# A new order for the steps of attention, of slot 0 and of the expert tables

## The chip, the cores and the metric

The kernel runs on one core of a Trainium2 chip. A core has five engines with queues of their own: PE (TensorE, matmuls and transposes; PEld is its loading of weights), DVE (VectorE), ACT (ScalarE), POOL (GpSimd) and SP, which here only issues transfers. The engines run side by side, each through its own list of instructions, and wait for each other by semaphores. The metric is the device time of the program in microseconds, the median of three runs.

## The reference

Three layers in a row, all in float32:

```python
scores = scale * np.matmul(q, k.transpose(0, 1, 3, 2))      # 2 x 12 heads, 448 x 448, D = 64
scores = np.where(mask, -1000000000.0, scores)              # causal
attn = np.exp(scores - np.max(scores, axis=-1, keepdims=True))
attn = attn / (np.sum(attn, axis=-1, keepdims=True) + 1e-09)
x = np.matmul(attn, v)                                      # -> 896 tokens x 768
expert_idx = np.argmax(xn @ en.T / tau, axis=1)             # 8 experts, top 1
out[mask] = gate_w[mask, None] * (np.maximum(x[mask] @ w1[e], 0.0) @ w2[e])   # 768 -> 1024 -> 768
h = np.maximum(np.maximum(x @ w1, x @ w2), x @ w3)          # last layer, 768 -> 768
return h @ w_out
```

## The kernel before, in words

Attention works on 12 pairs of heads (0 to 9, a, b; six for each of the two batches). The two heads of a pair stand in partitions 0 to 63 and 64 to 127. Queries come in 7 blocks i of 64 rows; block i sees 64 (i + 1) key columns, and the blocks are put into four groups that share a PSUM bank each: SG = ((6,), (5, 0), (4, 1), (3, 2)). The order in which all engines' instructions are issued is written out by hand in SCHEDULE, a list of words, and `emit` (the loop over SCHEDULE[:-1]) turns each word into instructions. Since each engine runs its own list, a word's place matters only against the other words of its engine, and by what it waits for. The first letter is the pair, then:

- S, Z: scores of a group's first and second block (`scores`, L503). Each matmul takes 64 rows and 64 columns of the array, a quarter. Head j lies in rows 64 j and writes to columns 64 (j xor SWAP[i]): SWAP is 0 for groups 0 and 1 and 1 for groups 2 and 3, so that the former use one diagonal of the array's quarters and the latter the other. A letter at the end (a, b, t, h) names the PSUM bank's tag.
- K: the causal mask added by a matmul (`masks`, L511). M: the rows' maxima on DVE (`row_max`, L515). E: exponentials with row sums on ACT (`row_exp`, L522). R: reciprocals on DVE (`row_rec`, L527 and L528).
- N: normalisation of a block's rows (`nrm`, L532), on DVE, or on POOL with a p behind it.
- T: transposes of the probabilities in 14 blocks of 128 x 128, in four steps (`ptr`, L542); t copies them out, on ACT (s) or DVE (v) (`ptr_out`, L476 or L478).
- A0 to A3: probabilities times values (`av`, L580 to L590). A0 to A2 use all 128 rows and half of the columns for each head, A3 only rows 0 to 63. a copies the output out, X transposes it to tokens (L599), x copies that out (s or v) and stores it on POOL's queue (L605).
- q scales the keys, L and V load on SP.

Words without a pair are steps that occur once: EA (norms of the expert embeddings on ACT, with two loads of activation tables, L143 and L144), ET, GA to GS1 and G4, G5 (logits of the experts), C0 and C1 (choice of experts for each batch, on DVE, L641 to L646), F1 to F3 (the first expert to run), XG (gather of its tokens), LW (a small transfer that holds the weights back until the gather has landed), L0, L1, L11, L13 (weights of slot 0), W (splits of these weights on ACT and DVE, L261 and L263), X0, X4 (transposes of slot 0's tokens) and H (slot 0's first layer, L272). The last string orders the tables of all further slots and slot 0's second layer (Y, L979): cnt, rk and iv are matmuls, P0 and P1 transposes of slot 0's hidden values (L328), sel, pb, A0 and A1 (here one-hot rows) and others are small DVE steps, J is the first layer of slot 1. Behind that the order is that of loops: up to 15 slots of 128 tokens, each with one expert, and then the last layer. None of that part is touched.

Of the kernel before, what the change touches and what calls it, by code (L numbers as in the profile page):

```python
# [15 lines left out]


SCHEDULE = (
    "0qv 0S0a 0S3 0S2b 0K0 0M0 0E0 0Z3 0K3 0M3 0S1b 0Z1 0Z2 0K2 0K1 1qv 0M2 0E3 4L 1S0a 1S3a 1Z3 1K3 0E2 0M1 1K0 1M0 0E1 1E0 1S2 1S1 1Z1 1K1 1Z2 1K2 5L 2qv 2S0b 2S3b 2Z3 2K0 2K3 2S2a 2S1 1M1 1E1 2Z2 2K2 0R 0N1p 1M3",
    "1E3 0N0 1M2 1E2 0N3 2Z1 2K1 0N4 0N2p 0T0t 0N5p 0N6 0T2 0t0s 3qs 0t2s 0T3h 0t3s 2M1 3S0 3S2 1R 3Z2 1N4p 2M3 2E3 3K2 1N3 0T1 2M2 2E2 0t1s 3S3h 1N2 1N1p 2M0 3K0 3M0 1N5p 3S1b 3Z3 3Z1 2E0 3K3 3M3 2E1 0A0a 0A2 0A1",  # L20
    "3M2 1N6p 1N0 2R 2N0p 2N5p 0A3 4V 2N1 6L 2N6p 1T0 1T2b 1t0v 4qs 1T3t 0as 1t2v 3E3 2N2 3K1 3M1 3E2 1t3v 2N3p 5qv 1T1 1t1s 2N4 4S0h 4S3a 3E1 4Z3 4K3 4M3 1A0t 1A2 3E0 1A1 3R 3N0p 3N3p 1A3 1av 5V 3N1p 4S2a 4K0 5S0b 4Z2",
    "2T0t 2T3t 2T1b 4M0 EA 2t0v 2T2t 2t3s 3N4p 6qv 2t2v 3N2p 4K2 4M2 4E3 3N5p 5S3 7L 7qv 4S1 2t1s 5Z3 5K3 4E2 5K0 4Z1 4K1 4M1 2A0a 2A1 3N6 2A2 5M0 4E0 4E1 2A3 6V 2as 3T0t 3T2h 3T1 3t0s 5M3 3T3t 5S1b 5E3 4R 4N3p 4N1p 4N5p",
    "5S2a 5Z2 3t2v 5E0 3t1v 5Z1 5K1 4N4p 5K2 5M1 6S0 6S3h 6Z3 5M2 3t3s 5E1 5E2 8L 6S1 4N6 4N0p 8qs 6S2b 6K3 6Z2 4N2 6Z1 6K1 6M1 6K0 6M0 6K2 3A0a 3A1 3A2 5R 5N4p 3A3 4T0 4T3b 7V 9L 6M3 5N0 5N1 3as 5N2p 4T1t 4t0s",
    "5N5p 5N3 4T2 4t3s 6E3 7S0b 4t2s 7S2a 7Z2 7K2 4t1v 4A0t 4A2 4A1 5N6p 7S3a 6E0 6M2 7K0 8S0 6E1 6E2 9qs 7M2 7Z3 7K3 6R 6N2p 6N3 4A3 8K0 8V aL 6N0 5T0h 5T2b 6N6 5t0s 6N1p 6N5p 8M0 7M3 5t2s 7M0 5T1t 5t1s 0Xh",
    "7S1b 7Z1 7E2 7K1 5T3t 5t3v 7E3 6N4p 5A0a 0xs 5A1 7E0 5A2 6T0h 6T1 8S2b 7M1 EM 7E1 8S1 7R 7N2p 6t1s 7N6 6t0s 7N5p 8Z2 8K2 6T3b 6t3s 6T2 7N3 1Xh 8Z1 8K1 8E0 aqv 1xs 7N4p 5A3 9S0 8S3b 8Z3 6t2s 8K3 8M2 6A0a 6A1",
    "8M1 8E2 8E1 6A2 8M3 9K0 9M0 7N1p 9V bL 8E3 ET 2Xh 7T0t 2xs 7t0s 3X 7T3b 7t3s GA 4as 9S1b 5as 8R 8N4p 6A3 aV 8N3 9Z1 9K1 GB 8N1p 7N0 7T2 4Xt 3xs GE0 9M1 7t2s 6as 7T1b GS0 9E0 7t1s 5Xt C0",
    "8N5p 7A0a 7A2 8N6p 4xs 8N2 F1 8T0 9E1 6Xt 9S3 9Z3 9K3 8t0s 7A3 7A1 9S2a 9Z2 9K2 F2 8N0p 6xs 9M2 7as 5xs F3 bV bqs RE 9M3 7Xt 8T3 8T2h XG 8t3v 9E2 8t2s 8T1t 8t1s aS0b aS2a aZ2 aK2 aK0 aS1a aS3b aZ3 aM2 aZ1 aK1",
    "aM0 9E3 bS0 9R bS2h bZ2 aE2 bS3 aM1 9N2p 9N0 9N6p 9N5 bZ3 bK3 aE0 9N3 aE1 9N1 aK3 aM3 9N4 bK2 7xs LW 8A0a 8A1 8A2 aE3 9T0b bM2 9t0s aR aN5p aN4 9T1t aN1p bK0 L0 8A3 9t1s aN0 8as bM0 9T2 9t2v X4 X4h X4l X0 X0h 9T3",
    "9t3v bE2 bE0 X0l bM3 bE3 bS1 bZ1 bK1 bM1 bE1 aN2 9A0a 9A1 9A2 aN6 L1 9A3 9as 8Xt W000h aN3p bR aT0t aT2b aT3t bN3 at3s at2s W001h bN5p bN2 bN0 at0s bN6 bN1 aT1 at1s GC 9X 8xv W010h GE1 bN4 bT0 bT2b bT1t bT3 W011h",
    "W010l aA0t aA1 bt1s W000l aA2 bt3v H00 aA3 W011l W021h bt2v aas GS1 G4 W001l aX W020h W020l H01 H04 H10 W030h bt0s W030l bA0a bA1 W031h W101h bA2 W021l 9xv W101l bA3 bav H02 H03 H05 L11 H13 W031l W100h G5 W100l W121h",  # L30
    "W121l W120h axs R0 H11 H12 H14 W110h L13 W120l C1 bXt bxs W110l",
    "rk ro cnt n8p rr g87 ge nb8 ks8 pre8 H15 rks B0 P0 U02 jj sb8 A0 sbo P0h P0l Y00 R1 Y10 W111h sl sl2 sel pb W131h P1 A1 pp iv Y11 Y13 nsf flg idx Y12 Y01 Y02 nsc P1h W130h P1l Y03 Y05 Y04 W130l inc st2 U03 st1 st3 st4 U11 st5 ti0 st6 W111l U10 Y06 xg1 x0 st7 x0h ti1 W131l RG x0l Y07 Y15 WS0 U00 Y16 U13 U01 q6 U12 x4 Y14 Y17 q3 q4 q5 x4h x4l q7 q8 q9 qb qc S1 qd qa qe qf B1 n8 J00 J10 J11 J02 J01 J03 J04 J05 J12 J14 r0 qh0 qg qh2 p0 qh1 gg p0h gx gs0 J13 J15 gs1 WS1 of0 of1 of2 y0 y1 p0l of3 of4 ti2 r1 RG1",
)


# [1132 lines left out]
```

## Time and profile before

| | |
|---|---|
| median of 3 runs (lowest, highest) | 471.49 us (471.2, 472.02) |
| profiled execution: its own time, its span | 473.37 us, 471.7 us |
| TensorE's mean granted clock | 0.999 of full speed |
| busy: PE, DVE, ACT, POOL | 459.0, 319.1, 269.1, 76.0 us |
| first score matmul, last step of pair b (X) | 5.74 us, 103.37 us |
| first matmul of slot 1 (J00) | 117.85 us |

The profile is that of one execution; all starts are in microseconds from the start of its span. The times of a group of instructions are durations from start to end, and those of neighbours overlap, since the engines are pipelined; what a stretch of an engine costs is read from start to start. In a line of the timeline, instructions of one form that lie close are merged (x12), and the bracket at the end gives the idle time in front and what ended it.

### The profile page before, as it was taken

Reading aid. Unit: us, or ns where it says so; the run is one execution under the profiler, and the core shown is the slowest. Engines: PE = TensorE matmul, PEld = TensorE weight load, DVE = VectorE, ACT = ScalarE, POOL = GpSimd, SP = SyncE. Lnnn points to the kernel's source line nnn. Section 1 sums busy time; section 2 is a strip of 40 time slices with the busy share of each in tenths; the row PEclk is TensorE's granted clock in tenths of the full one; section 3 lists DMA queues with packets and bytes.
Section 4 is the critical chain, followed back from the end, with each engine's and each line's share of the span. In section 5 each row is a group of like instructions: output and inputs, shape, how many; then the busy total and the mean of one; then the engine's idle time right before and its main releaser. Section 6 shows DMA issues by size and latency. Waiting matters only on the chain. (4 is left out here: it accounts for less than half of the span.)

```text
span 471.7 us, 9404 instructions
## 1 busy us (share of the span) xinstructions
PE 459.0 (97%) x3266; PEld 406.4 (86%) x3266; DVE 319.1 (68%) x642; ACT 269.1 (57%) x564; POOL 76.0 (16%) x101
## 2 busy tenths in 40 slices
PE   7999999999999999999999999999999999999994
PEld 6777777788899898998998987989989989899993
DVE  4987668887446794533978955898989889840000
ACT  5998878957627895335888954544444353410000
POOL 3877756111010000000000000000000000001111
PEclk9999999999999999999999999999999999999999
DMA  7444345931158891217999903844534330000111
GB/s 256 157 136 134 123 138 167 350 141 55 36 196 326 300 374 44 103 34 287 358 337 361 362 7 142 332 140 152 175 137 146 123 135 0 0 1 33 68 68 68
DMA packets 18175, 76.65 MB, mean 163 GB/s; under 512 B 2362, under 2 KB 5434, under 8 KB 18114
## 3 DMA queue, kind: packets, MB, share of 16 engines
q1 hardware_dynamic: 15410, 65.84, 39.1%
q0 software_dynamic: 2400, 9.83, 5.8%
q8 instruction: 27, 0.44, 0.4%
q10 hardware_dynamic: 304, 0.25, 0.2%
q14 instruction: 34, 0.28, 0.2%
...
## 5 line engine op out<-in xcount | busy, mean ns | idle before, releaser
L973 PE MATMUL pm<-x2h,dwh 128*128 128x512 f32 (+1 forms) x204 | 74.1, 363 | 0.0
L974 PE MATMUL pm<-x2l,dwh 128*128 128x512 f32 (+1 forms) x204 | 74.0, 363 | 0.0
L975 PE MATMUL pm<-x2h,dwl 128*128 128x512 f32 (+1 forms) x204 | 74.0, 363 | 0.0
L979 PE MATMUL l<-w2h,hh 128*128 128x384 f32 x160 | 55.3, 346 | 0.7 <-ACT hh L208 0.7
L979 PE MATMUL l<-w2l,hh 128*128 128x384 f32 x160 | 54.1, 338 | 0.0
L243 DVE TENSOR_TENSOR w1l<-raw,w1h 128x768 fp32r<-128x768 f32 x40 | 36.0, 953 | 21.8 <-ACT w1h L242 16.5
L532 POOL TENSOR_SCALAR prb<-prb,smq 128x384 f32<-128x384 f32 (+6 forms) x45 | 44.3, 1000 | 19.7 <-DVE smq L528 11.2
L175 ACT CAST dwh<-dt_t 128x768 fp32r<-128x768 f32 (+1 forms) x20 | 15.5, 774 | 53.5 <-DVE dt_t L174 53.5
L979 PE MATMUL l<-w1h,xhp 128*128 128x512 f32 x109 | 44.0, 404 | 0.0
L979 PE MATMUL l<-w1l,xhp 128*128 128x512 f32 x109 | 43.1, 395 | 0.0
L522 ACT ACTIVATE prb<-pss,smq 128x64 f32<-128x64 f32 (+6 forms) x84 | 39.2, 494 | 5.7 <-DVE smq L515 3.9
L975 PEld LDWEIGHTS pm<-x2h,dwl 128*128 128x128 f32 x204 | 38.3, 188 | 4.0
L973 PEld LDWEIGHTS pm<-x2h,dwh 128*128 128x128 f32 x204 | 38.3, 188 | 4.0
L974 PEld LDWEIGHTS pm<-x2l,dwh 128*128 128x128 f32 x204 | 38.3, 188 | 4.0
L1119 POOL DMA_INDIRECT out_dram<-ob,sidx x7 | 6.8, 976 | 195.1 <-DVE ob L1118 195.1
L979 PE MATMUL l<-w2h,hl 128*128 128x384 f32 x160 | 36.6, 338 | 0.1
L515 DVE TENSOR_REDUCE smq<-pss 128x1 f32<-128x256 f32 (+6 forms) x84 | 30.8, 413 | 8.6 <-PE pss L511 8.5
L199 POOL DMA_INDIRECT xrp<-xd,idx x11 | 11.2, 1019 | 152.1 <-PE xtp L217 144.4
L243 DVE TENSOR_TENSOR w2l<-raw,w2h 128x768 fp32r<-128x768 f32 x40 | 35.3, 955 | 0.4 <-ACT w2h L242 0.4
L242 ACT CAST w2h<-raw 128x768 fp32r<-128x768 f32 x40 | 30.5, 841 | 4.7 <-SPq L352 2.6
L242 ACT CAST w1h<-raw 128x768 fp32r<-128x768 f32 x40 | 31.7, 853 | 0.0
L979 PEld LDWEIGHTS l<-w2h,hh 128*128 128x128 f32 x160 | 30.1, 188 | 1.6 <-ACT hh L208 1.0
(260 smaller groups left out, 1004.4 us busy)
## 6 DMA issues: line engine op xcount, KB each, us to landing
...
```

The costliest lines, as they stand in the source:

```text
L175: nc.scalar.copy(out=hi[:, c0:c1], in_=f)
L199: nc.gpsimd.indirect_dma_start(out=xrp, out_offset=None, in_=xd if i else xd[0:S], in_offset=bass.IndirectOffsetOnAxis(ap=idx[:, i:i + 1] ...
L242: nc.scalar.copy(out=hi[:, sl], in_=r[:, sl])
L243: nc.vector.tensor_tensor(out=lo[:, sl], in0=r[:, sl], in1=hi[:, sl], op=ALU.subtract)
L515: nc.vector.tensor_reduce(out=sms[p][:, 0, SC[i]:SC[i] + 1], in_=held["s", p, g][:, SO[i]:SO[i] + 64 * (i + 1)], axis=AX.X, op=ALU.max, ne ...
L522: nc.scalar.activation(out=prb[p % 2][:, poff[i]:poff[i] + n], in_=ps[:, SO[i]:SO[i] + n], func=AF.Exp, bias=sm[:, 0, SC[i]:SC[i] + 1], sc ...
L532: eng.tensor_scalar(out=r, in0=r, scalar1=sms[p][:, 2, SC[i]:SC[i] + 1], scalar2=None, op0=ALU.mult)
L973: nc.tensor.matmul(o, lhsT=lh, rhs=rh, start=first, stop=False)
L974: nc.tensor.matmul(o, lhsT=lh, rhs=rl, start=False, stop=False)
L975: nc.tensor.matmul(o, lhsT=ll, rhs=rh, start=False, stop=last)
L979: nc.tensor.matmul(o, lhsT=a, rhs=b, start=first and n == 0, stop=last and n == len(ops) - 1)
L1119: nc.gpsimd.indirect_dma_start(out=out, out_offset=bass.IndirectOffsetOnAxis(ap=sidx[:, t:t + 1], axis=0), in_=ob, in_offset=None)
```

## The change

SCHEDULE is replaced. Both lists hold the same 735 words apart from their last letters: 6 of the 84 normalisations change from POOL to DVE on balance (45 to 39 on POOL), copies change between ACT and DVE, and PSUM tags change. Nothing else in the kernel differs.

```diff
@@ -16,20 +16,19 @@
 SCHEDULE = (
-    "0qv 0S0a 0S3 0S2b 0K0 0M0 0E0 0Z3 0K3 0M3 0S1b 0Z1 0Z2 0K2 0K1 1qv 0M2 0E3 4L 1S0a 1S3a 1Z3 1K3 0E2 0M1 1K0 1M0 0E1 1E0 1S2 1S1 1Z1 1K1 1Z2 1K2 5L 2qv 2S0b 2S3b 2Z3 2K0 2K3 2S2a 2S1 1M1 1E1 2Z2 2K2 0R 0N1p 1M3",
-    "1E3 0N0 1M2 1E2 0N3 2Z1 2K1 0N4 0N2p 0T0t 0N5p 0N6 0T2 0t0s 3qs 0t2s 0T3h 0t3s 2M1 3S0 3S2 1R 3Z2 1N4p 2M3 2E3 3K2 1N3 0T1 2M2 2E2 0t1s 3S3h 1N2 1N1p 2M0 3K0 3M0 1N5p 3S1b 3Z3 3Z1 2E0 3K3 3M3 2E1 0A0a 0A2 0A1",
-    "3M2 1N6p 1N0 2R 2N0p 2N5p 0A3 4V 2N1 6L 2N6p 1T0 1T2b 1t0v 4qs 1T3t 0as 1t2v 3E3 2N2 3K1 3M1 3E2 1t3v 2N3p 5qv 1T1 1t1s 2N4 4S0h 4S3a 3E1 4Z3 4K3 4M3 1A0t 1A2 3E0 1A1 3R 3N0p 3N3p 1A3 1av 5V 3N1p 4S2a 4K0 5S0b 4Z2",
-    "2T0t 2T3t 2T1b 4M0 EA 2t0v 2T2t 2t3s 3N4p 6qv 2t2v 3N2p 4K2 4M2 4E3 3N5p 5S3 7L 7qv 4S1 2t1s 5Z3 5K3 4E2 5K0 4Z1 4K1 4M1 2A0a 2A1 3N6 2A2 5M0 4E0 4E1 2A3 6V 2as 3T0t 3T2h 3T1 3t0s 5M3 3T3t 5S1b 5E3 4R 4N3p 4N1p 4N5p",
-    "5S2a 5Z2 3t2v 5E0 3t1v 5Z1 5K1 4N4p 5K2 5M1 6S0 6S3h 6Z3 5M2 3t3s 5E1 5E2 8L 6S1 4N6 4N0p 8qs 6S2b 6K3 6Z2 4N2 6Z1 6K1 6M1 6K0 6M0 6K2 3A0a 3A1 3A2 5R 5N4p 3A3 4T0 4T3b 7V 9L 6M3 5N0 5N1 3as 5N2p 4T1t 4t0s",
-    "5N5p 5N3 4T2 4t3s 6E3 7S0b 4t2s 7S2a 7Z2 7K2 4t1v 4A0t 4A2 4A1 5N6p 7S3a 6E0 6M2 7K0 8S0 6E1 6E2 9qs 7M2 7Z3 7K3 6R 6N2p 6N3 4A3 8K0 8V aL 6N0 5T0h 5T2b 6N6 5t0s 6N1p 6N5p 8M0 7M3 5t2s 7M0 5T1t 5t1s 0Xh",
-    "7S1b 7Z1 7E2 7K1 5T3t 5t3v 7E3 6N4p 5A0a 0xs 5A1 7E0 5A2 6T0h 6T1 8S2b 7M1 EM 7E1 8S1 7R 7N2p 6t1s 7N6 6t0s 7N5p 8Z2 8K2 6T3b 6t3s 6T2 7N3 1Xh 8Z1 8K1 8E0 aqv 1xs 7N4p 5A3 9S0 8S3b 8Z3 6t2s 8K3 8M2 6A0a 6A1",
-    "8M1 8E2 8E1 6A2 8M3 9K0 9M0 7N1p 9V bL 8E3 ET 2Xh 7T0t 2xs 7t0s 3X 7T3b 7t3s GA 4as 9S1b 5as 8R 8N4p 6A3 aV 8N3 9Z1 9K1 GB 8N1p 7N0 7T2 4Xt 3xs GE0 9M1 7t2s 6as 7T1b GS0 9E0 7t1s 5Xt C0",
-    "8N5p 7A0a 7A2 8N6p 4xs 8N2 F1 8T0 9E1 6Xt 9S3 9Z3 9K3 8t0s 7A3 7A1 9S2a 9Z2 9K2 F2 8N0p 6xs 9M2 7as 5xs F3 bV bqs RE 9M3 7Xt 8T3 8T2h XG 8t3v 9E2 8t2s 8T1t 8t1s aS0b aS2a aZ2 aK2 aK0 aS1a aS3b aZ3 aM2 aZ1 aK1",
-    "aM0 9E3 bS0 9R bS2h bZ2 aE2 bS3 aM1 9N2p 9N0 9N6p 9N5 bZ3 bK3 aE0 9N3 aE1 9N1 aK3 aM3 9N4 bK2 7xs LW 8A0a 8A1 8A2 aE3 9T0b bM2 9t0s aR aN5p aN4 9T1t aN1p bK0 L0 8A3 9t1s aN0 8as bM0 9T2 9t2v X4 X4h X4l X0 X0h 9T3",
-    "9t3v bE2 bE0 X0l bM3 bE3 bS1 bZ1 bK1 bM1 bE1 aN2 9A0a 9A1 9A2 aN6 L1 9A3 9as 8Xt W000h aN3p bR aT0t aT2b aT3t bN3 at3s at2s W001h bN5p bN2 bN0 at0s bN6 bN1 aT1 at1s GC 9X 8xv W010h GE1 bN4 bT0 bT2b bT1t bT3 W011h",
-    "W010l aA0t aA1 bt1s W000l aA2 bt3v H00 aA3 W011l W021h bt2v aas GS1 G4 W001l aX W020h W020l H01 H04 H10 W030h bt0s W030l bA0a bA1 W031h W101h bA2 W021l 9xv W101l bA3 bav H02 H03 H05 L11 H13 W031l W100h G5 W100l W121h",
-    "W121l W120h axs R0 H11 H12 H14 W110h L13 W120l C1 bXt bxs W110l",
-    "rk ro cnt n8p rr g87 ge nb8 ks8 pre8 H15 rks B0 P0 U02 jj sb8 A0 sbo P0h P0l Y00 R1 Y10 W111h sl sl2 sel pb W131h P1 A1 pp iv Y11 Y13 nsf flg idx Y12 Y01 Y02 nsc P1h W130h P1l Y03 Y05 Y04 W130l inc st2 U03 st1 st3 st4 U11 st5 ti0 st6 W111l U10 Y06 xg1 x0 st7 x0h ti1 W131l RG x0l Y07 Y15 WS0 U00 Y16 U13 U01 q6 U12 x4 Y14 Y17 q3 q4 q5 x4h x4l q7 q8 q9 qb qc S1 qd qa qe qf B1 n8 J00 J10 J11 J02 J01 J03 J04 J05 J12 J14 r0 qh0 qg qh2 p0 qh1 gg p0h gx gs0 J13 J15 gs1 WS1 of0 of1 of2 y0 y1 p0l of3 of4 ti2 r1 RG1",
+    "0qv 0S0b 0S2a 0Z2 0K0 0M0 0K2 0M2 0S1 0Z1 0S3 1qv 0Z3 0K3 4L 0K1 1S0 1S2b 1Z2 1K2 0E0 0E2 1S3b 1Z3 0M3 0E3 0M1 0E1 1K0 1M2 1M0 2qs 1E0 1K3 1M3 1S1 1Z1 1K1 1E3 5L 1E2 0R 0N0p 2S0h 2S3 2Z3 2K3 2S1a 2S2 2Z2 1M1 0N4p",
+    "0N5 0N1 2Z1 0N3 1E1 2K2 2K0 2K1 0N2 0N6 3qv 0T0b 0T1 0t0s 2M3 0t1s 1R 1N0p 1N4p 2M1 0T2b 0t2s 1N3p 0T3t 0t3s 2M0 1N2 2E1 2M2 0A0 0A1 0A2 4qv 2E0 1N1 2E3 0A3 4V 6L 0av 3S0 3S3b 1N5p 3S2a 3Z3 3K3 1N6 3K0 3Z2 3K2 3M2",
+    "2E2 1T0 3M3 2R 2N3p 5qs 1T2t 2N4p 1t0s 3E2 2N1 3M0 1T1b 2N0 1T3t 1t2s 3S1a 3Z1 1t3s 3K1 3E0 4S0h 4S3a 3M1 3E1 4Z3 4K3 4K0 4S1 1t1v 2N5p 3E3 4M3 4S2 4Z2 4K2 1A0 1A1 4M2 2N2p 1A2 3R 3N6p 3N2p 2N6 4Z1 4K1 1A3 1av 5V",
+    "7L 2T0b 2T3 EA 3N1p 2T2t 2t2s 2t0v 2t3v 2T1b 2t1v 4E3 4M1 5S0b 5S2a 5Z2 5K2 3N3 4M0 4E0 2A0 2A2 3N4p 2A1 5K0 2A3 5M2 3N5 6V 8L 3T0 3T3t 3N0p 2av 4E2 6qv 3T2h 3T1t 4E1 3t3v 3t0s 5M0 5E0 4R 4N0p 4N3p 4N2 4N1p 4N6 5S1",
+    "5S3b 5Z3 3t1s 5Z1 5K1 5M1 5K3 4N4 3t2s 6S0a 5E1 6S2 6Z2 5E2 6K0 5M3 5E3 6K2 3A0 3A2 3A1 3A3 7V 7qs 4T0t 6M0 6M2 4t0v 4N5p 4T2 4t2v 4T1t 4T3h 6S1b 6S3 3as 6E2 4t1s 5R 5N2p 4t3s 6Z3 5N3p 5N6 7S0b 7S2a 6E0 8qv 6K3 6M3",
+    "5N4 5N1p 6E3 7Z2 9L 5N0 6Z1 6K1 6M1 5N5 4A0t 4A2 9qv 7S1 7S3h 7K2 7M2 7Z3 6E1 6R 7K0 7M0 6N1p 6N3 7Z1 7K1 6N4 7K3 4A3 5T0t 5T3 5t0s 5t3s 6N2 5T2b 7E2 6N6p 7M1 4A1 5t2s 6N0 EM 5T1t 8V 5t1s 0Xa 0xs 6T0 8S0 8S2b 8Z2",
+    "8K0 aL 7E0 5A0a 7E1 5A2 7M3 7E3 5A1 6t0v aqs 1Xa 7R 6N5p 7N0 7N6 6T3t 7N5 7N3p 6t3s 6T2h ET 1xs 7N2 6T1t 6t1v 5A3 8S3b 7N1p 9V bL 8S1a 8K2 8M0 6t2s 8E0 8M2 8Z3 8Z1 8K1 8M1 7N4p 8K3 8M3 GA 2Xt 8E2 7T0t 4av 5av 7T1b",
+    "2xs 8E3 3Xt 8E1 GB GE0 bqv 8R 8N2p 8N0 8N1p 6A0 8N4 6A1 6A2 7t1s 3xs 8N3p 9S0a 9S2a 7t0s 9Z2 9S1b 9K2 9K0 9Z1 6A3 9K1 8N6 8N5p 9M0 aV 6as GS0 4X 7T2t 9M1 7T3t 7t2s 5Xt C0 F1 F2 8T0t 4xs 9E1 7A0h 8t0s 6X 7A1 7t3s",
+    "7A2 9E0 9M2 6xs 5xs 9S3 9Z3 9K3 7A3 bV 7as F3 RE 9M3 8T3 8T2t 8T1b 8t2v XG 8t3s 9E2 8t1s aS0 aS3a aZ3 aK3 aM3 9E3 aE3 aK0 8A0t 8A2 8A1 aM0 aS1b 9R 9N2p 9N4p 9N3 9N6 9N0 9N1 aS2h aZ2 aZ1 aK1 aM1 aK2 aM2 aE0 8A3 8as",
+    "bS0 bS3a bS2 bK0 bS1a aE1 bM0 aE2 bZ2 bK2 bZ3 9N5 bZ1 bK1 bM1 aR aN2 LW bK3 aN4 bM3 9T0b 9T2t 9t0s aN6 aN1p 9T3h 9t3s 9T1b X4 9t2s aN3p bM2 9t1s X4h X4l 7Xh aN5 9A0t 9A1 9A2 9A3 9av bE1 bE3 bE2 aT0b aT3b at3s at0v",
+    "aT1 8Xt aN0 aT2 at1v at2v bE0 9X bR bN1p bN2p X0 7xs X0h GC aA0a bN5 aA1 L0 bN6 X0l bN4p aA2 W001h W001l aA3 bN3 W000h W000l GE1 W011h W011l bN0 W010h aas GS1 bT0 bT1t bT3b bt0v bt1v W010l 8xs H00 bT2 aXt bt2v G4",
+    "W021h W020h W020l W031h H01 bt3s 9xv H04 H02 bA0a bA1 bA2 W031l bA3 W021l W030h L1 L11 W100h W030l W100l bas H03 H05 W101h G5 R0 H10 H13 H11 H12 W101l axs W121h C1 W120h bXa H14 W121l W120l W110h L13 W110l bxs",
+    "cnt n8p rk ro H15 g87 rr rks nb8 ge pre8 ks8 B0 U02 P0 sb8 sbo sl jj P0h W130h sl2 P0l Y10 Y11 sel pp A0 U10 pb A1 inc st2 Y00 U11 nsf R1 iv idx Y13 flg nsc Y12 W111h st1 Y01 st3 st4 st5 P1 P1h ti0 W111l W131h Y02 Y03 st6 st7 P1l ti1 Y05 Y04 Y06 xg1 x0 U03 W130l W131l x0h RG Y15 Y07 x0l WS0 q6 Y16 U00 Y14 x4 U01 Y17 x4h U12 U13 q3 q4 q5 x4l q7 q8 q9 qb qc S1 qd qa qe qf B1 n8 qh0 J10 J11 J00 J02 J01 J03 J04 J05 r0 J12 J14 qg qh2 qh1 p0 p0h gg J13 gx gs0 gs1 J15 WS1 of0 y0 p0l of1 of2 of3 of4 ti2 y1 r1 RG1",
 )
```

## Rows read from the trace of the kernel before

**Rows 1.** The page's line of busy times, and PE's busy tenths in 40 slices.

```profile
PE 459.0 (97%) x3266; PEld 406.4 (86%) x3266; DVE 319.1 (68%) x642; ACT 269.1 (57%) x564; POOL 76.0 (16%) x101
...
PE   7999999999999999999999999999999999999994
```

**Rows 2.** Stretches: length; busy us PE, PEld, DVE, ACT, POOL (instructions); clock, DMA share, GB/s.

```profile
0.00:20.00 20.00, 16.80 (x250) 13.14 (x250) 13.31 (x43) 14.89 (x51) 10.96 (x29) 1.00 0.61 206
20.00:40.00 20.00, 19.56 (x304) 15.66 (x300) 17.92 (x50) 18.61 (x61) 14.88 (x17) 1.00 0.41 126
40.00:60.00 20.00, 20.00 (x279) 15.18 (x278) 12.17 (x39) 17.91 (x59) 15.01 (x16) 1.00 0.45 149
60.00:80.00 20.00, 19.59 (x263) 15.40 (x260) 15.13 (x61) 15.87 (x48) 12.32 (x14) 1.00 0.41 122
80.00:100.00 20.00, 19.57 (x204) 15.17 (x201) 17.10 (x32) 16.45 (x36) 4.36 (x5) 1.00 0.90 334
...
120.00:140.00 20.00, 20.00 (x131) 17.97 (x130) 10.81 (x46) 8.75 (x17) 1.41 (x1) 1.00 0.30 101
```

**Rows 3.** Waits of PE, 0 to 120 us: total, times, longest.

```profile
PE pss L503 <- DVE ktq L482: 0.8, 1, 0.8
PE l L979 <- ACT hh L208: 0.7, 1, 0.7
PE pst L542 <- DVE prb L532: 0.6, 2, 0.3
```

**Rows 4.** PE in order of time (start, duration, what), 45.7 to 46.85 us.

```profile
45.79 0.98 PE L503 MATMUL pss<-ktq,qt 64*64 64x384 f32 x8
...
46.76 0.33 PE L542 MATMUL pst<-ident,prb 128*128 128x128 f32 x1
```

**Rows 5.** The same view, 15.3 to 18.1 us.

```profile
15.46 0.99 PE L503 MATMUL pss<-ktq,qt 64*64 64x448 f32 x12 [0.15 <-ACT ktq L486]
...
16.44 0.66 PE L542 MATMUL pst<-ident,prb 128*128 128x128 f32 x4
```

**Rows 6.** The same view, 33.4 to 36.3 us.

```profile
33.52 0.99 PE L503 MATMUL pss<-ktq,qt 64*64 64x384 f32 x16
...
36.19 0.44 PE L580 MATMUL psa<-ptq,vr 128*64 128x256 f32 x2
```

**Rows 7.** The same view, 21.2 to 21.6 us.

```profile
21.30 0.25 PE L511 MATMUL pss<-maskb,identb 64*64 64x64 bf16 x4
21.48 0.33 PE L542 MATMUL pst<-ident,prb 128*128 128x128 f32 x1
```

**Rows 8.** All engines in order of time, 24 to 30.6 us.

```profile
26.95 1.28 ACT L144 ACT_TABLE_LOAD   x1
...
27.59 0.25 PE L511 MATMUL pss<-maskb,identb 64*64 64x64 bf16 x4
...
28.75 0.86 PE L503 MATMUL pss<-ktq,qt 64*64 64x384 f32 x8 [0.44 <-ACT ptq L478]
...
29.77 1.09 PE L580 MATMUL psa<-ptq,vr 128*64 128x256 f32 x12
```

**Rows 9.** DVE by line and form, 0 to 104 us: busy us, mean ns, idle before.

```profile
L476 DVE COPY ptq<-pst 128x512 f32<-128x512 f32 x9 | 6.0, 686 | 0.6 <-PE pst L542 0.2
...
L532 DVE TENSOR_SCALAR prb<-prb,smq 128x448 f32<-128x448 f32 x7 | 3.9, 561 | 0.0
L532 DVE TENSOR_SCALAR prb<-prb,smq 128x256 f32<-128x256 f32 x8 | 3.7, 460 | 0.1
...
L476 DVE COPY xtq<-psa 128x448 f32<-128x448 f32 x2 | 1.2, 624 | 0.7 <-PE psa L590 0.7
...
L532 DVE TENSOR_SCALAR prb<-prb,smq 128x384 f32<-128x384 f32 x1 | 0.5, 546 | 0.0
```

**Rows 10.** DVE in order of time, 5 to 30 and 60 to 64.5 us.

```profile
7.22 1.22 DVE L515 TENSOR_REDUCE smq<-pss 128x1 f32<-128x448 f32 x3 [2.29 <-PE pss L511]
...
62.67 0.25 DVE L641 TENSOR_SCALAR lsc<-lgp,rtau 112x32 f32<-112x32 f32 x1 [2.34 <-PE lgp L629]
```

## The prediction

> **What bounds the kernel now.** I read the page's totals first: TensorE's matmuls are busy for 97% of the span, and PE's line of 40 slices (11.8 us each) shows a nine in all of them but the first and the last [rows 1]. The table of stretches then says where the missing 3% lie and who else is loaded: from 120 us on PE is busy in every microsecond, with DVE and ACT at about half. Whatever is won before 120 us is therefore handed on to the end, and nothing can be won behind it by an order of attention [rows 2]. In the attention (0 to 104 us) PE is also near full, and ACT is close behind it from 20 to 60 us, at 18.61 and 17.91 of 20 us. DVE has gaps there: 12.17 of 20 us from 40 to 60 us. The list of waits names few for PE, the largest one 0.8 us at the second pair's key scaling and 0.7 us at slot 0's first transposed activations [rows 3]. So a new order has two ways to gain: less time on PE for the same matmuls, and the few waits.
>
> How can the same matmuls take less time? The score matmuls use a quarter of the array each (64 rows by 64 columns), two at a time for the two heads. Groups 0 and 1 use one diagonal of quarters, groups 2 and 3 the other (SWAP). I call the diagonals halves, and a stretch of score, mask and A3 steps between two steps that need the full height of the array (T, X, A0 to A2, H, G) a run. Per pair each half has 896 columns; I count 448 as one unit (S0, or S1+Z1, or S2+Z2, or S3+Z3). A run with one unit in one half alone, 7S1 7Z1 7K1, lasts from 45.79 to 46.76, that is 0.97 us [rows 4]. A run with one unit in each half, 3S0 3S2 3Z2 3K2, lasts from 15.46 to 16.44, 0.98 us [rows 5]. The second half is free. A run with three units in each, 5S1 to 6K2, lasts from 33.52 to 36.19, 2.67 us [rows 6]. So a run costs 0.12 us and 0.85 us for every unit in its longer half ((2.67 - 0.97) / 2 = 0.85).
>
> **The change part by part.** Its name speaks of a decode that is gone, but both lists hold the same 735 steps, none of them a decode. What differs is the order, 6 of 84 normalisations that change from POOL to DVE on balance, the engine of some copies, and PSUM banks. Nothing is added or removed on PE or among the transfers.
>
> PE's packing. I went down both lists and closed a run at every full-height step. An A3 step adds 128 columns (0.29 unit) to the run that it stands in, since it uses only rows 0 to 63. Before: 26 runs, the longer halves add up to 30.57 units. After: 19 runs, 29.43 units. Examples of what is joined: 3S0 3S2 3Z2 and 3S3 3S1 3Z3 3Z1, two runs around 0T1, become parts of runs that also hold 0A3 and pair 4; the lone 3K1, 9K0 and 8A3 become parts of others; 7S1 7Z1, alone in its half, now stands beside 7S3 7Z3. Worth: 1.14 units x 0.85 = 0.97 us, and 7 runs x 0.12 = 0.84 us, together 1.8 us. The split between unit and fixed part is uncertain: the lone masks 3K1 hold PE from 21.30 to 21.48, 0.18 us [rows 7]; as the fixed part that leaves 0.79 for a unit and gives 0.9 + 7 x 0.18 = 2.2 us, and with no fixed part only the 1.0 us is left. I take 1.8, ends 1.0 and 2.2.
>
> The Trainium skill speaks against this term. Its page "TensorE: Matmul & The Clock Gate" (section "The mechanism") says that matmuls start and end strictly in program order. By that rule the second half's first pass would have to wait for the second pass of the first half, and pairing would pay about half as much. Rows 4 and 5 disagree, since the paired run is no longer than the single one, so I keep the 1.8 us and carry the rule as a rival.
>
> The step EA (two table loads on ACT of 1.28 us each, with the embedding's norms). In the kernel before, the run 4K2 5S3 4S1 that follows it lasts from 27.59 to 29.77, 2.18 us for one unit; 1.2 us more than its 0.97, and the row of 28.75 says that PE waited for an ACT copy queued behind EA [rows 8]. After, PE has behind EA 2T2, 2T1, a one-unit run of pair 5, 2A0 and 2A2 before 2A1 needs a copy that stands behind EA on ACT, and those that the others need are on DVE (2t0, 2t3, 2t1). I put the wait between 0 and 1.2 us and take half of it away, 0.6 us, since 4E3 and its bank also queue behind EA.
>
> The start: the order of the first three pairs differs, but PE waits there for the scaling 1q on DVE (0.8 us), which follows two row maxima in both lists; 2q moves from DVE to ACT, where the exponentials run without a pause. Cost between -0.3 and +0.5 us, taken as 0 because pair 0's four transposes and A steps end at about the same point of ACT's work in both lists.
>
> DVE, ACT and POOL. By the rows of each form DVE gets, in the attention, 6 more normalisations of 384 columns (0.546 us), 3 more of 448 (0.561) and 3 fewer of 256 (0.460): +3.6 us; 4 more outputs of A (0.624): +2.5; and 5 more copies of 512 columns (0.686): +3.4 [rows 9]. Three fewer copies of half that size take off 1.0 (an estimate from the same row), one more scaling and one copy of X less about cancel. Sum +8.5 us on DVE, while ACT loses the outputs and copies and POOL the normalisations. DVE was busy 75.6 us of the first 100 (five stretches of [rows 2]), so there is room, and I cost this at nothing beside PE's matmuls; what it costs without that cover is the slower rival below.
>
> The tables and slot 0 (from 104 to 118 us). The same steps; the wait of 0.7 us for slot 0's first hh [rows 3] stays, since P0 is still followed by a layer-2 step that reads it. The inversion iv now has three layer-2 steps ahead of it instead of two and P1, against DVE's sel, A0, pb and A1: 0 to +0.5 us. I take 0, as the first four column blocks need only A0. No load moves past another on SP: its order (k, q, v, mark, weights) is the same, and POOL's stores keep their order, so transfers come at most as much earlier as PE does.
>
> Sum: -1.8 - 0.6 = -2.4 us. The profiled execution took 473.37 us, 1.67 more than its span, so it would come to 471.0; the median of the three runs is 471.49, 1.9 below it, and -2.4 on that gives 469.1 us.
>
> **The rivals.** (a) All waits go: beside the 1.8 us the whole 1.2 us at EA, and PE's largest waits of the attention (the key scaling 0.8, the normalised rows 0.6 [rows 3]), 4.4 us together: 467.1. For it: ACT, close to full before, has 4 outputs and some copies less. Against: in a chain of scores, maxima, exponentials and transposes an order that removes one wait mostly makes another.
>
> (b) The packing is given back: PE reaches its steps 1.8 us earlier, and waits there for exponentials or normalisations that come no earlier. For it: ACT at 18.61 and 17.91 of 20 us from 20 to 60 us [rows 2]. Against: ACT has less to do after. 471.5.
>
> (c) Slower: DVE becomes the bound from pair 2 to the choice of experts for batch 0 (step C0, 62.67 us). Ahead of C0 the new list puts 8 more normalisations on DVE (about 0.5 each: 4.0), the 4 outputs of A (2.5) and the scaling (0.5), 7.0 us. In the first 60 us DVE is busy 43.4 [rows 2], idle 16.6, of which nearly 7 lie ahead of its first maximum at 7.22 [rows 10]; 9.8 are left, 2.3 of them in one wait just ahead of C0. The 7.0 us fit if DVE can do with 2.8 us of idle time. If its order forces it to keep half, 4.9, C0 and everything behind it come 2.1 us later than now: 473.6. Against it: most of that idle time is DVE waiting for PE's scores, and goes by itself once DVE is behind.
>
> (d) The quarters take turns: if matmuls kept strict order, the packing's unit term would halve, to 0.5 us, and the sum to -1.9: 469.6.
>
> **How the numbers follow.** Forecast (469.1, own range 467.8 to 470.5) 0.45; (a) 0.13; (b) 0.22; (c) 0.15; (d) 0.05. About 0.2%, 0.94 us, is what a measurement of this kernel can tell from no change. Faster: 0.45 + 0.13 + 0.05 = 0.63; the same: 0.22; slower: 0.15. The range goes from 466.5, below which I leave a little of (a), to 472.8, above which lies most of (c).
>
> **What would show it.** Right: the first layer-1 matmul of slot 1 (118 us before) comes 2 to 3 us earlier, and so does everything after it; runs such as 6S1 6S3 7S0 7S2 cost 0.12 + 0.85 x units; no wait of PE for an ACT copy near EA; DVE over 80 us busy in the first 100. Packing wrong: paired runs cost more than single ones. (b): PE's waits in the attention grow by as much as the runs shrink. (c): PE waits for normalisations or copies on DVE before 64 us, and DVE has hardly an idle stretch there. If the attention's end moves but the total doesn't, the reading that all behind 120 us is PE alone is wrong.

## The result: 4.25 us faster, and the profile after

| | before | after |
|---|---|---|
| median (lowest, highest) | 471.4 us (471.2, 472.02) | 467.15 us (467.02, 468.02) |
| ratio of the times, 95% interval | | 0.9905 [0.9893, 0.9917] |
| profiled execution: its own time, its span | 473.37, 471.7 us | 468.02, 466.3 us |
| last transpose of pair b (word bX), its start | 103.69 us | 99.42 us |
| first transposes of slot 1's own hidden values (word p0; "slot 1" below) | 124.72 us | 121.07 us |
| one slot of 128 tokens, mean over the loop | 18.99 us | 18.77 us |
| first matmul of the last layer's main loop | 298.86 us | 293.50 us |

"Slot 1" is the mark by which the kernels are compared here: what lies ahead of it is the attention, the choice of experts and slot 0; behind it the list of PE's waits names one more, 0.8 us at the entry of the last layer in either kernel. (The quoted expectations call this mark "the transposes of slot 0".) Line numbers of the kernel after are those of before less one (L503 is L502, L542 is L541, L979 is L978).

The page's totals of the kernel after (beside [rows 1]: PE 459.0 us, DVE 319.1, ACT 269.1, POOL 76.0):

```profile
PE 454.4 (97%) x3266; PEld 404.8 (87%) x3266; DVE 322.5 (69%) x654; ACT 265.9 (57%) x558; POOL 67.5 (14%) x95
```

The number of PE's instructions is the same; DVE has 12 more, ACT and POOL 6 fewer each. The stretches of the kernel after (columns as in [rows 2]):

```profile
0.00:20.00 20.00, 16.80 (x245) 13.66 (x246) 12.74 (x41) 14.82 (x51) 9.01 (x28) 1.00 0.66 214
20.00:40.00 20.00, 19.88 (x303) 16.27 (x303) 18.21 (x52) 19.52 (x65) 11.95 (x14) 1.00 0.45 144
40.00:60.00 20.00, 20.00 (x301) 15.25 (x296) 15.97 (x51) 16.02 (x54) 13.48 (x16) 1.00 0.38 123
60.00:80.00 20.00, 19.51 (x285) 15.91 (x286) 16.58 (x67) 15.99 (x53) 8.78 (x10) 1.00 0.42 126
80.00:100.00 20.00, 20.00 (x182) 16.49 (x181) 19.65 (x35) 15.81 (x30) 5.78 (x7) 1.00 0.85 337
...
120.00:140.00 20.00, 20.00 (x131) 17.96 (x130) 9.29 (x39) 6.48 (x13) 1.47 (x1) 1.00 0.47 173
```

DVE's column adds up to 83.15 us over the first 100, where it was 75.6; but the first 100 us now hold some 3.6 us more of the program, and the page's total rose by 3.4 us only. From 40 to 60 us it rose from 12.17 to 15.97, and ACT fell from 17.91 to 16.02 at the same amount of work for PE. PE's waits over the first 120 us of the kernel after:

```profile
PE warm L715 <- POOL identb L101: 1.8, 1, 1.8
PE pss L502 <- DVE ktq L481: 0.8, 1, 0.8
PE l L978 <- ACT hh L207: 0.7, 1, 0.7
PE pst L541 <- POOL prb L531: 0.3, 1, 0.3
PE pst L541 <- DVE prb L531: 0.3, 1, 0.3
PE pss L502 <- ACT ktq L485: 0.3, 1, 0.3
PE pst L541 <- ACT prb L521: 0.2, 1, 0.2
```

The 1.8 us lie ahead of the attention, where matmuls on an identity matrix (`warm`) fill PE, and stand in the list of before too, though the prediction calls 0.8 us the largest. The next two are those of before [rows 3]. The 0.44 us beside EA [rows 8] is gone; a new 0.3 us is that of the third pair's keys, now scaled on ACT (L485). PE by EA in the kernel after, with ACT and DVE between:

```profile
26.04 1.28 ACT L142 ACT_TABLE_LOAD   x1
...
26.32 1.75 PE L541 MATMUL pst<-ident,prb 128*128 128x128 f32 x14
...
27.01 1.78 DVE L475 COPY ptq<-pst 128x512 f32<-128x512 f32 x3
...
27.54 1.28 ACT L143 ACT_TABLE_LOAD   x1
...
27.99 1.07 PE L502 MATMUL pss<-ktq,qt 64*64 64x448 f32 x12
...
28.95 0.56 ACT L477 COPY ptq<-pst 128x512 f32<-128x512 f32 x1
29.05 1.52 PE L579 MATMUL psa<-ptq,vr 128*64 128x256 f32 x20
```

While ACT loads its tables, PE does all 14 transposes of pair 2 and the run 5S0 5S2, and DVE takes three of the four copies. The run lasts from 27.99 to 29.05, 1.06 us for one unit in each half; the run in the same place took 2.18 for one unit before [rows 8]. Further down, the run of 6S1 6S3 7S0 7S2, two units in its longer half, from its first matmul to the first of the A steps behind it:

```profile
38.58 1.61 PE L502 MATMUL pss<-ktq,qt 64*64 64x384 f32 x20
...
40.34 1.09 PE L579 MATMUL psa<-ptq,vr 128*64 128x256 f32 x12
```

1.76 us, where 0.12 + 2 x 0.85 = 1.82 was forecast.

**Where the attention's gain came from**, from start to start of PE's steps in the two profiled executions. From the first score matmul to the first step of the expert tables, the same steps in both: 98.07 to 94.50 us, -3.57:

| | before | after | difference |
|---|---|---|---|
| runs by the forecast's rule (0.12 us + 0.85 per unit) | 29.11 | 27.29 | -1.82 |
| excess of the first run (pairs 0 to 2), waits for keys in it | 2.17 | 2.83 | +0.66 |
| excess of the run behind EA | 1.21 | 0.09 | -1.12 |
| excess of all other runs | 0.37 | 0.53 | +0.16 |
| full-height steps (T, X, A0 to A2, H, G) with their waits | 65.20 | 63.76 | -1.44 |

The excess is what a run took beyond the rule. Another 0.1 us is won between there and slot 1, which comes 3.65 us earlier. The span is 5.4 us shorter; the other 1.7 us come from the pace of the slots, which is no effect of the change (last section).

### The profile page after: what moved, and what is told of

Same layout as the page of the kernel before. It is cut to its first block, busy times and chain, and to the rows that moved or that the text cites. A ratio compares the mean times of both kernels' runs of the same rounds, so it can differ in the third digit from the quotient of the medians.

```text
span 466.3 us, 9400 instructions
## 1 busy us (share of the span) xinstructions
PE 454.4 (97%) x3266; PEld 404.8 (87%) x3266; DVE 322.5 (69%) x654; ACT 265.9 (57%) x558; POOL 67.5 (14%) x95
## 5 line engine op out<-in xcount | busy, mean ns | idle before, releaser
L978 PE MATMUL l<-w2h,hh 128*128 128x384 f32 x160 | 55.1, 344 | 0.7 <-ACT hh L207 0.7
L978 PE MATMUL l<-w2l,hh 128*128 128x384 f32 x160 | 53.6, 335 | 0.0
L978 PE MATMUL l<-w1h,xhp 128*128 128x512 f32 x109 | 43.7, 401 | 0.0
L978 PE MATMUL l<-w1l,xhp 128*128 128x512 f32 x109 | 42.7, 392 | 0.0
L521 ACT ACTIVATE prb<-pss,smq 128x128 f32<-128x128 f32 (+6 forms) x84 | 39.2, 494 | 3.9 <-DVE smq L514 3.7
L531 POOL TENSOR_SCALAR prb<-prb,smq 128x128 f32<-128x128 f32 (+6 forms) x39 | 36.0, 940 | 28.1 <-DVE smq L527 12.2
L978 PE MATMUL l<-w2h,hl 128*128 128x384 f32 x160 | 36.4, 337 | 0.1
L514 DVE TENSOR_REDUCE smq<-pss 128x1 f32<-128x128 f32 (+6 forms) x84 | 30.3, 411 | 6.0 <-PE pss L510 5.9
L978 PEld LDWEIGHTS l<-w2h,hh 128*128 128x128 f32 x160 | 30.1, 188 | 1.6 <-ACT hh L207 1.0
```

The source lines that it names most:

```text
L514: nc.vector.tensor_reduce(out=sms[p][:, 0, SC[i]:SC[i] + 1], in_=held["s", p, g][:, SO[i]:SO[i] + 64 * (i + 1)], axis=AX.X, op=ALU.max, ne ...
L521: nc.scalar.activation(out=prb[p % 2][:, poff[i]:poff[i] + n], in_=ps[:, SO[i]:SO[i] + n], func=AF.Exp, bias=sm[:, 0, SC[i]:SC[i] + 1], sc ...
L531: eng.tensor_scalar(out=r, in0=r, scalar1=sms[p][:, 2, SC[i]:SC[i] + 1], scalar2=None, op0=ALU.mult)
L978: nc.tensor.matmul(o, lhsT=a, rhs=b, start=first and n == 0, stop=last and n == len(ops) - 1)
```

## Experiments

Each is compared with the kernel before, run on the same chip. "Slot 1" and the sums of runs are from the profile of one execution.

**The kernel after once more.** No edit; it shows how much two executions differ.

> The changed kernel once more, unaltered, for a narrower ratio and a second profile. Theory: PE's shorter runs and fewer waits before 104 us pass to the end. The first profiles differ by 3.7 us at the first matmul of slot 1 (117.85 before, 114.2 after) and by 5.4 us at the end; the timed medians differ by 4.25 us. If the 1.7 us that come on top in the slot loop (18.99 against 18.77 us a slot) belong to the change, this profile has 18.8 us a slot again and the unaltered kernel before has 19.0. If they belong to the single execution, one of the two moves.

467.08 us (466.93 to 468.62), before 472.2; ratio 0.9888 [0.9866, 0.991]. Slot 1 at 119.95 us. The runs other than the first (22.53 us, 22.70 in the first profile) and the full-height steps (63.74, 63.76) agree; the attention began at 5.33 instead of 5.74, and the first run took 7.48 instead of 8.05. Its slots took 18.99 us each.

> The kernel before, unaltered, one more profile. Theory that the slot loop's pace varies between executions: 18.8 us a slot this time, a span near 469.7 us. Rival, that the old order makes the slot loop slower: 19.0 us a slot and a span near 471.7 again.

A single execution, 474.0 us; slot 1 at 125.35, first run 7.91 us, 18.99 us a slot. So slot 1 gains 3.65 to 5.4 us by the pairs of these four profiles, and the first run's excess is not steady: 2.17 and 2.69 before, 2.83 and 2.26 after. The +0.66 above lies within that. The rest is steady: without the first run the attention took 90.68, 90.63 and 90.62 us in the old order (before, before_again and table_only below) and 86.45, 86.27 and 86.28 in the new one (after, after_again and attn_only), so the change wins 4.2 to 4.4 us there. With before_2t3v and after_split3, whose edits lie behind it, the first run has four profiles of either order, with means of 7.58 us before and 8.00 after: some 0.4 us are lost again.

**Attention alone, and tables alone.** attn_only has the new list with the old last string, table_only the old list with the new one.

```diff
 SCHEDULE = (   # attn_only: the new order, but for the last string
-    "cnt n8p rk ro H15 g87 rr rks nb8 ge ...
+    "rk ro cnt n8p rr g87 ge nb8 ks8 pre8 ...
```

> The new order for attention with the old one for tables and slot 0's second layer. Theory: the whole gain lies in the attention, so 467.2 us (within 0.5 of the changed kernel). Rival, that the new table order carries part of it (the timed gain is 0.6 us larger than what the traces differ by at the end of attention): 468 us or more.

468.93 us (468.03 to 470.48), ratio 0.993 [0.9906, 0.9954]. Slot 1 at 121.16 us, 0.09 from the kernel after.

> The old order of attention with the new one for tables and slot 0's second layer. Theory: no gain, 471.4 us within 0.4. Rival: 470.8 or less, if the table order carries part of the gain.

472.28 us (470.79 to 473.85), ratio 0.9997 [0.998, 1.0014]. Slot 1 at 124.60 us, 0.12 from before. All of the gain at slot 1 is the attention's; the tables' order gives nothing there. In the whole time attn_only missed the theory: it is 1.85 us slower than the kernel after on the same chip, in the range of its rival. In the profiled executions 1.0 us of that arises where DVE enters the last layer; the rest was not found. DVE's first instruction there, in the kernel after and in attn_only:

```profile
284.53 0.62 DVE L279 TENSOR_SCALAR y<-l,glast 128x384 f32<-128x384 f32 x1 [4.87 <-PEq L1014]
```

```profile
286.74 0.62 DVE L279 TENSOR_SCALAR y<-l,glast 128x384 f32<-128x384 f32 x1 [6.98 <-ACT x2h L203]
```

DVE left the slots' last branch at 284.06 and at 284.44 us, so it starts 0.5 us behind it in the one and 2.3 in the other, and PE's first six matmuls that need its x2l take 2.54 instead of 1.64 us. The same words in another order of the tables; what makes DVE late was not settled.

**2t3 on DVE in the kernel before.** The copy that the run behind EA waits for leaves ACT.

```diff
-2t0v 2T2t 2t3s
+2t0v 2T2t 2t3v
```

> The kernel before with one letter changed: the copy 2t3, which stood behind EA on ACT, goes to DVE. Theory: PE's run 4K2 5S3 4S1 lasts 1.0 to 1.1 us instead of 2.18, and slot 1 begins 1.1 to 1.2 us earlier; time about 1.1 us less than before, as PE is busy on the way to the end. Rival: the wait comes back at the next step that needs a product of ACT behind EA (4E3's bank, 2A1), and 0 to 0.4 us is won.

472.29 us, ratio 0.9988 [0.997, 1.0005]; slot 1 at 124.52, 0.2 earlier. The run shrinks from 2.18 to 1.75 us, and 0.56 of the 1.75 is now a wait of the step behind it. That is 0.4 us won, of which a first run 0.2 us longer, ahead of the edit, takes half back:

```profile
27.79 0.25 PE L511 MATMUL pss<-maskb,identb 64*64 64x64 bf16 x4
...
29.54 1.34 PE L580 MATMUL psa<-ptq,vr 128*64 128x256 f32 x16 [0.56 <-ACT prb L522]
```

The rival came true. What ACT does next stands behind EA, so a single copy moved away only shows the next product of ACT. The 1.2 us needed several steps of PE that ask nothing of ACT, which the new order puts there.

**Three paired runs cut.** In the kernel after, one transpose step is put into the middle of three runs, between their halves. No step is added.

```diff
-2t0v 2t3v 2T1b 2t1v 4E3 4M1 5S0b 5S2a
+2t0v 2t3v 5S0b 2T1b 2t1v 4E3 4M1 5S2a
-6T0 8S0 8S2b
+8S0 6T0 8S2b
-8T3 8T2t 8T1b 8t2v XG 8t3s 9E2 8t1s aS0 aS3a
+8T3 8T2t aS0 8T1b 8t2v XG 8t3s 9E2 8t1s aS3a
```

> The changed kernel with three runs of one unit in each half cut in two by one transpose step each (2T1, 8T1 and 6T0 put between the halves). Theory: each cut costs a whole run of one unit, 0.97 us, together +2.9 us at slot 1 and in the time. Rival, matmuls in strict order, so that a pair saves half: +1.6. Rival, PE has slack there and waits absorb it: under 1 us.

471.19 us (469.0 to 472.4), ratio 0.996 [0.994, 0.9981]. Slot 1 at 124.02, 2.95 us later than in the kernel after; the rule gave 3 x 0.97 = 2.91. PE at the first of the three cuts:

```profile
27.78 0.97 PE L502 MATMUL pss<-ktq,qt 64*64 64x448 f32 x4
28.68 0.66 PE L541 MATMUL pst<-ident,prb 128*128 128x128 f32 x4
29.27 0.97 PE L502 MATMUL pss<-ktq,qt 64*64 64x320 f32 x8
...
30.23 1.53 PE L579 MATMUL psa<-ptq,vr 128*64 128x256 f32 x20
```

0.90 and 0.96 us for the halves apart, 1.06 together. In all three places the runs lengthen by 2.57 us; of the steps that now stand in front of a run two (2T2, 8T2) take 0.09 us more each and one (0X) 0.45, and other waits shrink. The first run, which the edit doesn't touch, is 0.20 longer in this profile; without it the attention is 2.67 us longer than in the kernel after, and 2.85 longer than in its second profile. So the rule holds to 0.2 us here, and 2.95 against 2.91 agrees better than the parts do. The profiled spans, both at 18.77 us a slot, differ by 2.96 us (469.3 and 466.3). What the packing takes reaches the end, and on balance next to nothing of it is handed back in waits. (The medians differ by 4.0 us, the lowest times by 2.0.)

**No second half.** All score matmuls use one diagonal.

```diff
-SWAP = {i: int(g > 1) for g in range(4) for i in SG[g]}
+SWAP = {i: 0 for g in range(4) for i in SG[g]}
```

> The changed kernel with SWAP = 0 for all blocks: all score matmuls use one diagonal of the array's quarters, so no run has a second half. Theory: the runs' longer halves add up to 51.4 units instead of 29.4, 22 x 0.85 = +18.7 us, less the few waits that this covers (up to 2 us). Rival, strict order (pairing pays half): +9 us.

482.32 us, ratio 1.0198 [1.0162, 1.0234]; slot 1 at 133.97. The run 5S0 5S2 again:

```profile
31.70 1.73 PE L502 MATMUL pss<-ktq,qt 64*64 64x448 f32 x12
33.26 0.23 PE L510 MATMUL pss<-maskb,identb 64*64 64x64 bf16 x4
33.41 1.52 PE L579 MATMUL psa<-ptq,vr 128*64 128x384 f32 x16
```

1.71 us instead of 1.06. All runs add up to 45.09 us; the rule, with every unit in the one half, gives 45.99. From the 30.74 us of the kernel after that is +14.4, of which 1.5 come back as shorter waits of the transposes, and slot 1 is 12.9 later. That is 4 us less than the 16.7 to 18.7 expected, as the longer runs also cover the 3.45 us of waits that stood in the runs, but well above the 9 of strict order. (The edit also merges matmuls of A0 to A2, 288 instead of 336; their stretch stays the same, 20.55 and 20.56 us.) A slower PE hides waits that a faster one shows; the reverse of this is why the forecast's rival (b) was worth a chance.

**2q back on DVE.** The third pair's keys, as before.

```diff
-1M0 2qs 1E0
+1M0 2qv 1E0
```

> The changed kernel with the scaling 2q on DVE again, as before. Theory: the first run (5.7 us to the first transpose) got 0.6 us longer because 2q stands behind pair 0's exponentials on ACT; it shortens by 0.4 to 0.7 us, and the time by as much. Rival: the later maxima on DVE push R and the first normalisations back, and the first transposes wait for what the run wins: 0, or slower by up to 0.4.

468.53 us (467.18 to 470.28), ratio 0.991 [0.9884, 0.9937]. Slot 1 at 120.37, 0.7 earlier than in the first profile of the kernel after (0.24 of it in the first run) and 0.4 later than in the second, but the time is not better: DVE enters the last layer late again, at 286.17 us.

**The same, with 9q on ACT in exchange.**

```diff
-1M0 2qs 1E0 ... 4A0t 4A2 9qv 7S1
+1M0 2qv 1E0 ... 4A0t 4A2 9qs 7S1
```

> The kernel after with the third pair's scaling (2q) on DVE, as before, and in exchange 9q on ACT, so that DVE has as many instructions as in the kernel after. Theory (the first run of the attention lost 0.7 us to 2q behind ACT's exponentials; the late entry of DVE into the last layer, which took this gain back when 2q alone was moved, hangs on where DVE's instructions lie): the transposes of slot 0 at 120.2 to 120.6 us instead of 121.07; if the last layer is entered as in the kernel after, the time is 466.3 to 466.8 us; if it is entered late again, 467.4 to 468.5. Rival (9q on ACT costs what 2q gave): 121 us, 467.1.

468.48 us (467.15 to 469.4), ratio 0.9922 [0.9901, 0.9943]. In the profiled execution, the fastest of its six, slot 1 came at 120.18 (0.26 us of the 0.89 because the attention began earlier), DVE entered the last layer in time (283.67), and the span was 465.5. The median is not below the kernel after's 467.15. Both profiles lie between the two of the kernel after at slot 1 (121.07 and 119.95), so that a cost of 2q there is not shown, and no version was found that is faster than the kernel after.

**Order and engines apart.** after_eng_before has the new order, with each normalisation, copy, scaling and output of A on its engine of before; before_eng_after is the reverse.

```diff
-2qs ... 0N0p ... 0N4p 0N5 0N1 ... 3qv ... 2t2s 2t0v 2t3v ... 2t1v
+2qv ... 0N0 ... 0N4 0N5p 0N1p ... 3qs ... 2t2v 2t0v 2t3s ... 2t1s
```

> The order of the kernel after, but each normalisation, copy, scaling and output of A on the engine that it had before. The runs on PE are those of the kernel after. Theory (the order carries the gain): the runs still sum to 27.3 us; of the waits some come back, most likely beside EA, where 2t3 and 2t1 stand on ACT behind the table loads again (0.5 to 1.2 us), so the transposes of slot 0 come 0.3 to 2 us later than in the kernel after (121.07 there, 124.72 before): 121.4 to 123.1 us, time 467.5 to 469.5 us. Rival (the relief of ACT carries the gain): 124 us or later, time 470.5 to 472.

480.96 us (480.37 to 481.04), ratio 1.0185 [1.0161, 1.0208]; slot 1 at 133.98. My theory and its rival were both wrong, in time by 9 us and more. The runs by the rule are the 27.29 of the kernel after, yet PE waits in them (33.20 us instead of 30.74) and above all between them (74.21 us of full-height steps instead of 63.76). Its waits over the first 40 us:

```profile
PE pst L541 <- POOL prb L531: 2.4, 3, 1.2
PE warm L715 <- POOL identb L101: 1.8, 1, 1.8
PE psa L579 <- ACT ptq L477: 1.2, 1, 1.2
PE pss L502 <- PE pst L541: 1.0, 1, 1.0
PE pss L502 <- DVE ktq L481: 1.0, 2, 0.8
PE pss L502 <- ACT prb L521: 0.6, 2, 0.4
```

> The order of the kernel before, with each normalisation, copy, scaling and output of A on the engine that it has after; DVE gets its 8 us more. The runs on PE are those of the kernel before (29.1 us). Theory: nothing gained, 0 to 1.5 us lost, since the copies were put where the new order has room: the transposes of slot 0 at 124.5 to 126.2 us, time 471.3 to 473. Rival (the relief of ACT carries the gain): 122 to 123.5 us, time 468.5 to 470. Rival (DVE becomes the bound once it has the work): 127 us or more, time 474 or more, with PE waiting for normalisations and copies of DVE.

481.66 us (480.14 to 483.78), ratio 1.0205 [1.0174, 1.0237]; slot 1 at 135.01, 10.3 later than before. The largest of its waits for POOL stands at bT0, from 80 to 122 us:

```profile
PE pst L542 <- POOL prb L532: 2.4, 1, 2.4
```

A part of the 10.3 us is a lower clock. PE waited up to 93.45 us there, and at 94.6 TensorE's granted clock fell to its lower level (1.2 GHz) for 3.4 us, and 3.4 us later once more; in no other profile here did it fall between the first 8 and the last 5 us. Stretches with columns as in [rows 2], and the steps A0 to A2 of a pair, first at the lower and then at the full clock (2.4 GHz):

```profile
90.00:94.60 4.60, 2.25 (x21) 1.81 (x18) 2.54 (x5) 2.38 (x4) 3.20 (x3) 1.00 1.01 394
94.60:98.00 3.40, 3.40 (x31) 2.52 (x29) 0.60 (x1) 0.00 (x0) 0.00 (x0) 0.50 0.53 212
98.00:101.40 3.40, 2.99 (x27) 2.14 (x25) 3.06 (x5) 2.33 (x5) 0.00 (x0) 1.00 0.24 33
101.40:104.80 3.40, 3.40 (x13) 2.99 (x14) 3.40 (x5) 2.23 (x4) 0.00 (x0) 0.50 0.86 325
```

```profile
94.95 2.40 PE L580 MATMUL psa<-ptq,vr 128*64 128x256 f32 x16
...
98.11 0.50 PE L272 MATMUL l<-w1h,xhp 128*128 128x512 f32 x1
...
105.89 1.31 PE L580 MATMUL psa<-ptq,vr 128*64 128x256 f32 x16
...
107.58 0.45 PE L590 MATMUL psa<-ptq,vr 64*64 64x64 f32 x8
```

3.16 us instead of 1.69; and five matmuls of slot 0 from 102.59 on take 2.27 us, where five take 1.15 at the 0.23 each of the kernel before. So the two stretches cost some 2.6 us (an estimate from these rows), and the other 7.7 us at slot 1 are mostly waits. The two of the four executions whose mean clock is 0.994 or more took 480.14 and 480.77 us, the other two 482.56 and 483.78.

This is the third outcome that I had named in size (slot 1 at 127 us or later) but not in cause: it isn't DVE alone that PE waits for. The list of waits up to 122 us gives POOL's normalisations 3.3 us, ACT's keys and probabilities 3.5, DVE's keys, copies, weights and normalisations 2.4. Neither the order nor the engine choice holds any gain by itself. Each alone loses 8 to 10 us against the kernel before; together they win 4.

**Only the normalisations back.** 23 go from DVE to POOL and 17 from POOL to DVE, in the new order.

> The kernel after, with only the 84 normalisations back on the engines that they had before (23 go from DVE to POOL, 17 from POOL to DVE); scalings, copies and outputs of A stay as after. With all engine choices of before the transposes of slot 0 came at 133.98 us instead of 121.07, 12.9 later. Theory (normalisations carry most of that, since one on POOL lasts about twice as long as one on DVE and a transpose waits for the last of its block): 127 to 131 us, time 473 to 477. Rival (copies and scalings behind ACT's exponentials carry it): 121.5 to 124 us, time 467.5 to 470.5.

472.33 us (471.14 to 474.32), ratio 0.9993 [0.9975, 1.001]; slot 1 at 125.54, 4.5 later than in the kernel after. That falls between what the two theories gave. PE's waits for POOL, 0 to 122 us:

```profile
PE pst L541 <- POOL prb L531: 3.3, 4, 1.2
```

The kernel after has one such wait of 0.3. A normalisation lasts longer on POOL, and the transpose waits for the last one of its block:

```profile
L531 POOL TENSOR_SCALAR prb<-prb,smq 128x256 f32<-128x256 f32 x7 | 7.0, 994 | 2.4 <-PE pst L541 1.9 <-DVE smq L527 0.5
...
L531 POOL TENSOR_SCALAR prb<-prb,smq 128x448 f32<-128x448 f32 x2 | 2.9, 1431 | 0.5 <-DVE smq L527 0.5
```

```profile
L531 DVE TENSOR_SCALAR prb<-prb,smq 128x448 f32<-128x448 f32 x10 | 4.7, 466 | 0.0
L531 DVE TENSOR_SCALAR prb<-prb,smq 128x384 f32<-128x384 f32 x7 | 3.0, 429 | 0.0
...
L531 DVE TENSOR_SCALAR prb<-prb,smq 128x256 f32<-128x256 f32 x5 | 2.3, 453 | 0.0
```

994 and 1431 ns on POOL and 453 and 466 on DVE (kernel after), where DVE took 460 and 561 before [rows 9]. So which of the 84 normalisations POOL does, and that they are 45 instead of 39, is worth 4.5 of the 12.9 us; the other 8.4 hang on copies, scalings and outputs, or on both together, which was not taken apart further.

## Why the prediction was right in sign and 2 us short

The time fell, and lies in the range given, but below the 467.8 to 470.5 of the likeliest case, and slot 1 came 3.65 us earlier where 2 to 3 were named. By its own steps:

- **What bounds the kernel.** Right: PE is as full as before behind slot 1, and 2.95 us put into the attention came out at the end of the profiled span as 2.96 (after_split3).
- **PE's packing, -1.8.** Right. The rule's own sum over the lists is -1.82; the runs other than the first and the one behind EA fell from 23.29 to 21.64 us in the first profiles, -1.65, and to 21.47 in the second of the kernel after. Both experiments bear the rule out: three cuts cost 2.7 to 2.9 where it gives 2.91, and without the second half the runs add up to 45.09 where it gives 45.99. The Trainium skill ("TensorE: Matmul & The Clock Gate", section "The mechanism") says that matmuls start and end strictly in program order. By that rule, as the prediction estimates it, the second half would be worth about half as much; the trace disagrees, with 1.71 us for the run on one diagonal (after_noswap) and 1.06 on two. Rival (d), the price of strict order, falls by the same two numbers and by the three cuts, for which it gave 1.6 us.
- **The wait behind EA, -0.6.** Mis-sized: 1.12 of 1.21 us went. Right were the steps named (2T2, 2T1, the run of pair 5, copies on DVE); the half was taken off for 4E3 and its bank, which hold up nothing in the profile after.
- **The start, 0.** The first run is 0.66 us longer in the first pair of profiles, above the bound of +0.5; over four profiles of either order it is some 0.4 longer. Moving 2q back took 0.24 us off it, which is less than executions of one kernel differ by (8.05 and 7.48).
- **What the forecast left out: the full-height steps.** They fell by 1.44 us, in each of three profiles of either attention (65.16 to 65.20, and 63.74 to 63.76), and I had no term for them. A part, some 0.3 us, belongs to the packing: fewer of these steps stand in front of a run, where a transpose step takes 0.53 us instead of 0.44. The larger part is waits. The list of waits [rows 3] gives PE's waits for normalised rows as 0.6 us, while the starts of T, X and H steps, each against the shortest of its kind with the same step behind it, show some 2.9 us of excess before and 1.8 after, counting those over 0.12. The row understates them, since PE counts as busy while neighbouring matmuls are still in flight. Which of the changes took these waits away was not tried on its own; nor were the PSUM tags.
- **DVE's 8.5 us at nothing.** Up to the expert tables DVE's instructions add up to 92.3 us before and 97.7 after, 5.4 more. Copies (+3.4) and outputs (+2.5) came as costed, but the normalisations grew by 1.4 instead of 3.6: one of 384 columns takes 0.429 us, where the single row of before had 0.546. That the first 100 us hold over 80 us of DVE, as named, is partly luck, since they hold more of the program now. Rival (c) didn't come. But the reason given, room on DVE, is not the one that decides: with its old order and the same work on DVE the kernel loses 8 to 10 us, so the cover is that each moved product has its place in the order.
- **The tables, 0.** Right: 0.1 us at slot 1 either way.
- **The rivals.** (a) gave 467.1, next to the measured 467.15, but that is luck: of its waits, the key scaling's 0.8 us is still there and that for normalised rows is still 0.6 in sum by the list; only EA's went. (b) is refuted: the full-height steps fell instead of growing by what the runs shrink, and after_split3 shows no cover for the reverse.

What the sum had wrong is thus its second term and the missing third: -1.1 and -1.4 in place of -0.6 and 0, against +0.8 in the runs. Worked out again that is -1.8 - 1.1 - 1.4 + 0.8 - 0.1 = -3.6 at slot 1 for the first pair of profiles. The medians differ by 4.25 us, and by 5.1 when both kernels were measured again (467.08 and 472.2); what lies beyond the 3.6 is not attributed, and executions of the kernel before alone lie between 470.9 and 474.1.
